# A fused attention and gated feed-forward kernel: logit sums by accumulating transfers instead of matmuls, first weights in halves, last store from ScalarE

## The chip, the core and the metric

The kernel runs on one core of a Trainium2 chip. Five engines run their own instruction streams, each strictly in its own order: TensorE (PE, matmuls into PSUM; PEld is its weight load), VectorE (DVE), ScalarE (ACT), GpSimd (POOL) and SyncE (SP). SP, ScalarE and GpSimd also issue transfers (DMA), which 16 DMA engines carry out. Engines wait for one another by semaphores. The metric is the device time of the program in microseconds; smaller is better.

## The reference

x is 2048 rows of 512. xn is its LayerNorm, and the result is x + s * g: s is a local dilated attention of xn with 32 heads of 16, g is silu of a gated feed-forward of xn.

```python
    W, dil = 8, 2
    qkv = (xn @ wqkv) ...                        # q, k, v: 32 heads of 16
    idx = pos[:, None] - arange(W) * dil         # position, and 2, 4, .. 14 before it
    logits = einsum("bhsd,bhswd->bhsw", q, kg) * scale      # masked below position 0
    attn = softmax(logits)                        # over the 8 places
    s = einsum("bhsw,bhswd->bhsd", attn, vg) ... @ wo
    g = silu((gelu(xn @ w_gate) * (xn @ w_up)) @ w_down)    # 512 -> 1792 -> 512
    return x + s * g
```

## The kernel before

The 2048 positions are four blocks of 512 (`TQ`, block j), each of four tiles of 128. Python functions record operations (`self.op(name, engine, duration, needs, emit, ...)`), each with estimated duration, the operations that it needs, buffers that it takes and a priority. `schedule` (line 75) then plays a list scheduler over them: at each step it picks the operation that can start first on its engine, by priority among those within 0.05 us, and so fixes each engine's order and the slot of every buffer. The order of `PARAMS` (lines 55 to 60) enters by per-stage base priorities and a seeded jitter. The program is then emitted in that order; on the chip each engine follows its own stream and waits for its semaphores.

For each block: `layernorm` (222) takes mean and variance (by ScalarE for the blocks in `sums`, else by DVE), normalizes, and turns the block to features x positions (`xnT`), by PE for block 0 and by transposing transfers from SP for the others. `qkv` (418; `qkv_tiles`, 503, for block 0) makes q, k and v. v goes through DRAM (`vT_dram`) and comes back with 4 x 32 partitions, quadrant tq holding the 32 heads of the tile tq of the block (`v_loads`, 562). `scores` (582) multiplies q with eight shifted windows of k on DVE: the four chunks c of q and k hold four of the 16 head features each, a head on four neighbouring partitions. Two levels of adds on DVE (`ladd`) sum the four chunks. What is left is a sum over the four partitions of each head, which PE does as a matmul with a 128x32 matrix of ones (`ind`):

```python
nc.tensor.matmul(
    L[H * tq : H * (tq + 1), w2, :], lhsT=self.ind[:],
    rhs=self.t[f"pr{j}_{w2}_{c}"][:, :, tq * P : (tq + 1) * P],
```

Eight such matmuls a block (line 640) fill two PSUM banks (pool "L"), laid out as 4 quadrants of 32 heads. The max over the eight places (`peak`), the subtraction (`less`), the exponential, its sum, reciprocal and scaling follow (656 to 690). `values` (708) multiplies the weights with eight windows of v and adds the products pairwise on DVE, one of the sums as an accumulating transfer from GpSimd (725). `turned` (849) takes the result through DRAM to features x positions, and `out` (871) multiplies it with wo (`s_ps`, line 883), multiplies with silu of the feed-forward, adds x and stores. `ffn` (752) makes the gate (`g_ps`) and up (`u_ps`) products with gelu, copies and products into `hT`; `down` (808) multiplies with w_down (`y_ps`, line 823) and takes silu. PSUM has eight banks: six in pool "F" that all matmul groups share, two for the logit sums. `loads` (964) issues all loads from SP but the second half of the first x tile.

Of the kernel before, what the change touches and what calls it, by code (L numbers as in the profile page):

```python
# [39 lines left out]
TABLE = 1.29  # L40
START = 0.8
LAT = {"PE": 0.2, "DVE": 0.1, "ACT": 0.13, "POOL": 0.15}
DEPENDENT = 0.115
DMA_FIXED = 2.3
DMA_CROWDED = 3.5
LOADED = 42.0
DMA_RATE = {"SP": 325e3, "POOL": 180e3}

POOLS = {"F": 6, "L": 1, "q": 2, "k": 2, "pr": 9, "attn": 2, "Ls": 1, "v": 2, "o": 1, "oT": 1, "h": 1,
         "xT": 2, "gl": 3, "sil": 1, "s16": 1, "xn": 4, "vst": 4}  # L50


DMA_SUMS = {(0, 0)}

PARAMS = dict(
    sums=(2, 3), ladd=2, ln_act=3, warm=4, slack=2.94, jitter=(9069, 1.0), N=[-49.4, -9.8, 21.5, 188.1],
    S=[108.2, -30.7, 42.8, 79.5], V=[-15.6, 90.4, 135.0, 139.5], Q=[-51.4, 66.2, 79.4, 143.2],
    F=[-41.0, 82.0, 126.2, 195.4], Y=[60.3, 103.2, 181.0, 249.0], O=[41.6, 84.1, 218.1, 258.6],
# [3 lines left out]
class Op:  # L62
    __slots__ = ("name", "eng", "dur", "need", "emit", "take", "use", "prio", "table", "bytes",
                 "start", "done", "end", "n", "slack", "mode")

    def __init__(self, name, eng, dur, need, emit, take=(), use=(), prio=0.0, table=None, nbytes=0,
                 slack=0.0, mode="full"):
# [4 lines left out]
        self.mode = mode  # L72


def schedule(ops, pools):
# [3 lines left out]
    for i, o in enumerate(ops):  # L79
        o.n = i  # L80
        waits[o.name] = len(o.need)
        for d in o.need:
            nexts[d].append(o.name)
# [10 lines left out]
    wire = {"SP": 0.0, "POOL": 0.0}  # L94
# [7 lines left out]
    while any(ready.values()):  # L102
# [31 lines left out]
        if o.bytes:  # L134
            clock[e] = t + o.dur
            wire[e] = max(wire[e], t + o.dur / 2) + o.bytes / DMA_RATE[e]
            end = wire[e] + DMA_FIXED + (DMA_CROWDED if e == "POOL" and t < LOADED else 0.0)
# [11 lines left out]
        o.done = end if o.bytes else clock[e] + (DEPENDENT if e == "DVE" else 0.0)  # L149
# [7 lines left out]
        for n in nexts[o.name]:  # L157
            waits[n] -= 1
            if not waits[n]:
                at[n] = max(  # L160
                    by[d].done if by[d].eng == by[n].eng else by[d].end + by[n].slack for d in by[n].need
                )
                ready[by[n].eng].append(by[n])
# [4 lines left out]
class Kernel:  # L168


    def __init__(self, par=PARAMS):
        self.par = par
        self.ops = []
        self.t = {}
        self.sums = {}
# [46 lines left out]
    def layernorm(self, j):  # L222
        base = self.when("N", j)
        for tt in range(TPB):
            t = j * TPB + tt
            prio = base + 2.0 * tt if j else -50.0 + tt
# [5 lines left out]
            def aggr(t=t):  # L232
                nc = self.nc
                nc.vector.bn_aggr(out=self.mv[:, t, :], in_=self.stats[:, t, :])

# [8 lines left out]
            def shift(a, b):  # L244
                self.nc.vector.scalar_tensor_tensor(
                    out=self.nmr[:, a:b, 0], in0=self.mv[:, a:b, 0], scalar=-1.0, in1=self.rstd[:, a:b, 0],
                    op0=ALU.mult, op1=ALU.mult,
                )
# [14 lines left out]
            def norm_dve(t=t):  # L263
# [4 lines left out]
                    scalar2=self.rstd[:, t, :], op0=ALU.subtract, op1=ALU.mult,  # L268
# [16 lines left out]
            def copy(t=t, tt=tt, j=j):  # L285
# [3 lines left out]
                if t == 1:  # L289
# [7 lines left out]
            by_act = j in self.par["sums"]  # L297
            if by_act:
# [14 lines left out]
                self.op(f"aggr{t}", "ACT", 0.70, [f"mean{t}"], square, prio=prio)  # L313
            else:
                self.op(f"stats{t}", "DVE", 0.61,
                        [f"ld_x{t if j == 0 else j}_{j}"] + {1: ["aggr0"], 2: ["copy1"]}.get(t, []), stats, prio=prio,
                        slack=(0.0, 0.5, 3.0, 3.0)[j])
                self.op(f"aggr{t}", "DVE", 0.16, [f"stats{t}"], aggr, prio=prio)
            on_act = j > 0 or t >= self.par["ln_act"]
# [6 lines left out]
            else:  # L326
                a, b = j * TPB, (j + 1) * TPB
                if tt == 0:
# [4 lines left out]
                    self.op(f"rstd{j}_", "POOL", 3.0, need,  # L333
                            lambda f=power, a=a, b=b, k=1.0 / D if by_act else 1.0: f(a, b, k), prio=prio, slack=0.5)
                ready = f"rstd{j}_"
            if on_act:
                self.op(f"norm{t}", "ACT", 0.75, [ready], norm_act, take=[("xn", f"xn{t}")],
                        use=[f"xn{t}"], prio=prio, slack=3.0 if j else 0.0)
            else:
                self.op(f"norm{t}", "DVE", 0.34, [ready], norm_dve, take=[("xn", f"xn{t}")],  # L340
                        use=[f"xn{t}"], prio=prio)
            if j:

                def cross(t=t, tt=tt, j=j):
                    if tt == 0:
# [5 lines left out]
                self.op(f"copy{t}", "SP", 0.8, [f"norm{t}"] + ([f"copy{t - tt}"] if tt else []), cross,  # L351
                        take=[("xT", f"xT{j}")] if tt == 0 else [], use=[f"xn{t}", f"xT{j}"], prio=prio,
                        nbytes=P * D * 2)
# [5 lines left out]
            self.op(f"copy{t}", *(("DVE", 0.34) if t == 1 else ("ACT", 0.5)), need, copy, take=take, use=[f"tr{t}", f"xT{j}"], prio=prio)  # L359

    def first_tile(self):
# [30 lines left out]
        def copy(i):  # L392
# [3 lines left out]
            self.nc.scalar.activation(out=out, in_=self.t[f"tr0_{i}"][:], func=AF.Copy)  # L396
# [14 lines left out]
        self.op("copy0", "ACT", 0.28, ["turn0_1", "copy0_0"], lambda: copy(1), use=["tr0_1", "xT0"], prio=prio)  # L411
# [6 lines left out]
    def qkv(self, j):  # L418
# [6 lines left out]
        for which, c in groups:  # L425
# [45 lines left out]
            if which == 2:  # L471
# [7 lines left out]
                self.op(f"stv{j}_{c}", "POOL", 1.0, [f"ev_{key}"], store, use=[f"vst{j}_{c}"], nbytes=128 * 1024)  # L479
# [23 lines left out]
    def qkv_tiles(self, base):  # L503

        for t in range(TPB):
            for which in range(3):
                key = f"{'qkv'[which]}0_t{t}"

                def mms(t=t, which=which, key=key):
                    ps = self.new("ps_" + key, [P, NC, P], F32, "qkv_ps")  # L510
                    for c in range(NC):
                        for dk in range(NC):
# [3 lines left out]
                                start=(dk == 0), stop=(dk == NC - 1),  # L516
# [19 lines left out]
                def store(t=t):  # L536
# [5 lines left out]
                self.op(f"mm_{key}", "PE", NC * NC * MM128, [f"copy{t}", f"ld_w{'qkv'[which]}"], mms,  # L542
                        take=[("F", "ps_" + key)], use=["ps_" + key, "xT0"],
                        prio=base + (0.5 if (t, which) == (1, 0) else t * 2 + which if which < 2 else 8 + t))
# [12 lines left out]
                if which == 2:  # L557
                    self.op(f"stv0_{t}", "POOL", 1.0, [f"ev_v0_{t}"], store, use=[f"vst0_{t}"],
                            nbytes=128 * 1024)
        self.v_loads(0)  # L560

    def v_loads(self, j):
        for tq in range(TPB):
# [10 lines left out]
            need = [f"stv{i}_{c}" for i in (j - 1, j) if i >= 0 for c in range(NC)]  # L574
            if j == 0:
                need = [f"stv0_{t}" for t in range(tq + 1)]
            need += [f"ldv{j}_0"] if tq else []
            self.op(f"ldv{j}_{tq}", "POOL", 1.0, need, load, take=[("v", f"v{j}")] if tq == 0 else [],
                    use=[f"v{j}"], prio=1.0, nbytes=290 * 1024)


    def scores(self, j):
        base = self.when("S", j)
        ladd = self.par["ladd"]
        sums = {}
        k = 0
        for w2 in range(2):
            for c in range(NC):


                cuts = [(0, 2), (2, 4)] if j == 0 and w2 == 0 else [(0, 4)]
                before = []
                for a, b in cuts:

                    def prod(j=j, w2=w2, c=c, a=a * P, b=b * P):
                        nc = self.nc
                        if a == 0:
                            self.new(f"pr{j}_{w2}_{c}", [P, 4, TQ], BF16, "prod")
                        off = PAD - HALO + 8 * w2 + a
                        win = self.t[f"k{j}"][:, c, off : off + b - a]  # L600
                        win = bass.AP(tensor=win.tensor, offset=win.offset, ap=[win.ap[0], [2, 4], [1, b - a]])
                        nc.vector.tensor_tensor(  # L602
                            out=self.t[f"pr{j}_{w2}_{c}"][:, :, a:b],
                            in0=self.t[f"q{j}"][:, c, a:b].unsqueeze(1).to_broadcast([P, 4, b - a]),
                            in1=win, op=ALU.mult,
                        )

                    need = [f"halo{j}"] + [f"ev_{n}{j}_{i}" for n in "qk" for i in ([c] if j else range(b))]
                    name = f"prod{j}_{w2}_{c}" + ("h" if b < TPB else "")
                    self.op(name, "DVE", 1.135 if b - a == 4 else 0.603, need + before, prod,  # L610
                            take=[("pr", f"pr{j}_{w2}_{c}")] if a == 0 else [],
                            use=[f"pr{j}_{w2}_{c}", f"q{j}", f"k{j}"], prio=base + k)
                    before = [name]
                k += 1

            def add(a, b, j=j, w2=w2):
                pa, pb = self.t[f"pr{j}_{w2}_{a}"], self.t[f"pr{j}_{w2}_{b}"]
                self.nc.vector.tensor_tensor(out=pa[:], in0=pa[:], in1=pb[:], op=ALU.add)  # L618

            tiles = [(c, f"prod{j}_{w2}_{c}") for c in range(NC)]  # L620
            step = 1
            for level in range(ladd):
                nxt = []
                for i in range(0, len(tiles), 2):
                    (a, na), (b, nb) = tiles[i], tiles[i + 1]
                    nm = self.op(f"ladd{j}_{w2}_{level}_{a}", "DVE", 1.135, [na, nb],
                                 lambda a=a, b=b, f=add: f(a, b),
                                 use=[f"pr{j}_{w2}_{a}", f"pr{j}_{w2}_{b}"], prio=base + k - 3)
                    nxt.append((a, nm))
                tiles = nxt  # L630

            sums[w2] = tiles

        def reduce(j=j):
            nc = self.nc
            L = self.new(f"L{j}", [P, 2, TQ], F32, "L_ps")
            for w2 in range(2):
                for i, (c, _) in enumerate(sums[w2]):
                    for tq in range(TPB):
                        nc.tensor.matmul(  # L640
# [489 lines left out]
```

## Time and profile before

| what | value |
|---|---|
| median of 3 runs (216.15 to 216.32) | 216.17 us |
| the profiled execution | 216.41 us |
| its span, first to last instruction | 214.7 us |
| granted TensorE clock | 1.0 throughout |
| first projection matmul starts | 6.31 us |
| last matmul ends | 210.57 us |
| instructions of PE, DVE, ACT, POOL | 1132, 216, 269, 69 |

The profile describes one execution. Busy time of an engine is the time in which it ran an instruction; the chain of waits follows back from the last instruction to what released it, at each step, and so names the work that the time consists of. A group of instructions is those of one line, engine and form, with the mean duration of one. For transfers, the time from issue to landing is given.

### The profile page before, as it was taken

How to read it: one execution, taken by the hardware profiler on the slowest of the kernel's cores; microseconds unless marked ns; L12 is line 12 of the kernel's file. 1: busy time of each engine (PE TensorE's matmuls, PEld its weight loads, DVE VectorE, ACT ScalarE, POOL GpSimd, SP SyncE). 2: the span in 40 equal slices, each digit the busy share in tenths (PEclk: the TensorE clock that was granted, in tenths of full speed). 3: DMA queues.
4: the chain of work that ended last, by engine and by line, in shares of the span. 5: the costliest groups of instructions: out<-in, count | busy, mean ns of one | idle time of the engine just before them, and what ended most of it. 6: DMA issues, size and time to landing. Idle time of an engine off the chain costs nothing.

```text
span 214.7 us, 3046 instructions
## 1 busy us (share of the span) xinstructions
PE 208.4 (97%) x1132; PEld 100.8 (47%) x1132; DVE 182.0 (85%) x216; ACT 156.4 (73%) x269; POOL 36.7 (17%) x69
## 2 busy tenths in 40 slices
PE   6999999999999999999999999999999999999992
PEld 2896444444544444444444444444444444444441
DVE  4598995599999999999999999999998799953033
ACT  3588999999998989877519967776724987765241
POOL 5036310034044312230200001001350010001000
PEclk9999999999999999999999999999999999999999
DMA  5999999204322401680297019303635540026712
GB/s 145 360 380 375 312 288 215 52 0 85 61 49 101 108 24 39 134 208 2 50 180 161 3 22 164 108 0 66 175 114 102 144 83 18 0 37 159 172 49 77
DMA packets 30575, 25.88 MB, mean 121 GB/s; under 512 B 16208, under 2 KB 28640, under 8 KB 30560
## 3 DMA queue, kind: packets, MB, share of 16 engines
q1 hardware_dynamic: 27584, 17.50, 31.4%
q0 software_dynamic: 2832, 8.11, 17.4%
q8 instruction: 9, 0.15, 0.3%
q14 instruction: 6, 0.05, 0.1%
q10 hardware_dynamic: 144, 0.07, 0.1%
HBM read 14.12 MB, written 6.31 MB: 95 GB/s over the span
## 4 chain that ended last, share of the span: by engine, by line
PE 93%; DMA 3%; SPq 1%; DVE 0%; ACT 0%; issue 0%; DVEq 0%
PE y_ps L823 23%; PE g_ps L763 23%; PE u_ps L763 23%; PE qkv_ps L432 15%; PE s_ps L883 6%; PE qkv_ps L513 3%; DMA wv_sb<-in_A_wqkv_dram 3%; PE L_ps L640 1%; SPq L968 1%; SPq L980 0%; DVE s L934 0%; ACT sil L838 0%; PE tr_ps L283 0%; DVE s L940 0%; DVEq L1125 0%
## 5 line engine op out<-in xcount | busy, mean ns | idle before, releaser
L763 PE MATMUL g_ps<-xnT,wg_sb 128*128 128x512 bf16 x224 | 56.0, 379 | 0.0
L763 PE MATMUL u_ps<-xnT,wu_sb 128*128 128x512 bf16 x224 | 55.4, 379 | 0.0
L823 PE MATMUL y_ps<-wd_sb,hT 128*128 128x512 bf16 x224 | 50.3, 379 | 0.0
L779 ACT ACTIVATE gl<-g_ps 128x512 bf16<-128x512 f32 x56 | 33.3, 602 | 9.7 <-PE g_ps L763 9.3
L602 DVE TENSOR_TENSOR prod<-q_sb,k_sb 128x2048 bf16<-128x2048 bf16 (+1 forms) x36 | 38.3, 1096 | 1.5 <-ACT k_sb L529 1.1
L787 ACT ACTIVATE hT<-u_ps 128x512 bf16<-128x512 f32 x56 | 33.2, 603 | 8.0 <-PE u_ps L763 7.9
L713 DVE TENSOR_TENSOR pv<-attn,v_arr 128x2048 bf16<-128x2048 bf16 x32 | 37.9, 1216 | 0.0
L823 PEld LDWEIGHTS <-hT 128*128 128x128 bf16 x224 | 21.7, 98 | 26.8 <-issue 0.8
L763 PEld LDWEIGHTS <-wu_sb 128*128 128x128 bf16 x224 | 21.9, 98 | 26.1
L763 PEld LDWEIGHTS <-wg_sb 128*128 128x128 bf16 x224 | 21.8, 98 | 26.2 <-issue 0.4
L618 DVE TENSOR_TENSOR prod<-prod 128x2048 bf16<-128x2048 bf16 x24 | 28.8, 1215 | 0.0
L721 DVE TENSOR_TENSOR pv<-pv 128x2048 bf16<-128x2048 bf16 x20 | 24.3, 1214 | 0.2
L801 DVE TENSOR_TENSOR hT<-hT,gl 128x1024 bf16<-128x1024 bf16 x28 | 19.0, 681 | 5.7 <-ACT hT L787 3.1
L838 ACT ACTIVATE sil<-y_ps 128x512 bf16<-128x512 f32 x16 | 9.4, 603 | 16.4 <-PE y_ps L823 16.3
L883 PE MATMUL s_ps<-wo_sb,oT_sb 128*128 128x512 bf16 (+2 forms) x68 | 15.0, 366 | 0.0
L897 ACT ACTIVATE s<-s_ps 128x512 bf16<-128x512 f32 x15 | 9.0, 597 | 5.7 <-PE s_ps L883 5.7
L569 POOL DMA_DIRECT2D v_arr<-vT_dram x16 | 10.5, 661 | 13.0 <-DMA vT_dram<-vst 12.8
L432 PE MATMUL qkv_ps<-xnT,wk_sb 128*128 128x512 bf16 x48 | 12.3, 379 | 0.0
L432 PE MATMUL qkv_ps<-xnT,wq_sb 128*128 128x512 bf16 x48 | 12.0, 379 | 0.0
L432 PE MATMUL qkv_ps<-xnT,wv_sb 128*128 128x512 bf16 x48 | 11.2, 379 | 0.0
L910 POOL DMA_DIRECT2D s<-x_sb x3 | 2.6, 875 | 50.1 <-DVE s L907 50.1
L274 ACT ACTIVATE xn<-x_sb,nmr,rstd 128x512 bf16<-128x512 bf16 x13 | 10.3, 827 | 0.0
(85 smaller groups left out, 196.6 us busy)
## 6 DMA issues: line engine op xcount, KB each, us to landing
v_arr<-vT_dram POOLq DMA_DIRECT2D x16, 142.0 KB, 4.0
vT_dram<-vst POOLq DMA_DIRECT2D x16, 128.0 KB, 2.3
pv<-pv POOLq DMA_DIRECT2D x4, 512.0 KB, 5.2
oT_dram<-o_sb SPq DMA_DIRECT2D x16, 128.0 KB, 2.8
oT_sb<-oT_dram SPq DMA_DIRECT2D x4, 512.0 KB, 3.6
wg_sb<-in_B_w_gate_dram SPq DMA_DIRECT2D x2, 896.0 KB, 10.8
wu_sb<-in_B_w_up_dram SPq DMA_DIRECT2D x2, 896.0 KB, 12.7
wd_sb<-in_B_w_down_dram SPq DMA_DIRECT2D x1, 1792.0 KB, 20.5
```

The costliest lines, as they stand in the source:

```text
L432: self.nc.tensor.matmul(ps[:], lhsT=self.w_qkv(which, dk, c), rhs=self.t[f"xT{j}"][:, dk, :], start=(dk == 0), stop=(dk == NC - 1),)
L569: self.nc.gpsimd.dma_start(out=self.t[f"v{j}"][H * tq : H * (tq + 1), :, :], in_=self.vT.rearrange("(h d) s -> h d s", d=DH)[:, :, a : a + ...
L602: nc.vector.tensor_tensor(out=self.t[f"pr{j}_{w2}_{c}"][:, :, a:b], in0=self.t[f"q{j}"][:, c, a:b].unsqueeze(1).to_broadcast([P, 4, b - a] ...
L618: self.nc.vector.tensor_tensor(out=pa[:], in0=pa[:], in1=pb[:], op=ALU.add)
L713: self.nc.vector.tensor_tensor(out=pv[:], in0=self.t[f"at{j}"][:, w, :].unsqueeze(1).to_broadcast([P, DH, P]), in1=self.t[f"v{j}"][:, :, 2 ...
L721: self.nc.vector.tensor_tensor(out=out[:], in0=pa[:], in1=pb[:], op=ALU.add)
L763: nc.tensor.matmul(ps[:], lhsT=w[:, dk, fc * P : (fc + 1) * P], rhs=self.t[f"xT{j}"][:, dk, :], start=(dk == 0), stop=(dk == NC - 1),)
L779: self.nc.scalar.activation(out=self.t[f"gl{j}_{pair}"][:, fc % 2, :], in_=self.t[f"ps_g{j}_{fc}"][:], func=AF.Gelu_apprx_tanh,)
L787: self.nc.scalar.activation(out=self.t[f"h{j}"][:, fc, :], in_=self.t[f"ps_u{j}_{fc}"][:], func=AF.Copy)
L801: self.nc.vector.tensor_tensor(out=h, in0=h, in1=self.t[f"gl{j}_{pair}"][:], op=ALU.mult)
L823: nc.tensor.matmul(self.t["ps_" + key][:, 0 : n1 - n0], lhsT=self.t[f"h{j}"][:, fc, tt * P : (tt + 1) * P], rhs=self.wd_sb[:, fc, n0:n1], ...
L883: self.nc.tensor.matmul(ps[:, 0 : n1 - n0], lhsT=self.t[f"oT{j}"][:, c, tt * P : (tt + 1) * P], rhs=self.wo_sb[:, c, n0:n1], start=(c == 0 ...
```

## The change

- `scores` is split. `logits` orders the products by halves of the block (n2: two tiles of 128) with all eight places in one instruction, instead of by halves of the places; three adds a half leave one tile `pr{j}_{n2}_0`. `reduced` is the matmul way of before, used for block 0 alone (`psum=(0,)`). `gathered`, for blocks 1 to 3, sums over the four partitions of a head by transfers from GpSimd: for each quadrant, four transfers of every fourth partition (32 x 1024 bf16) into `Ls` (32 partitions of fp32), the first a plain write, the other three accumulating. `peak` and `less` then read `Ls` in SBUF, in place.
- `values` makes four products of double width instead of eight; the accumulating transfer sums the two halves of the first.
- The first two y tiles of each block share the two banks of pool "L" as one tile (`shared=True`).
- Wq, wk and wv are loaded in halves, wq's from ScalarE's queue; w_down in two parts. In block 0, tile 0, the q and k matmuls are recorded as two operations of two feature chunks each, which need the halves. The second half of the first transposed tile is copied by DVE instead of ScalarE; tile 1's statistics are taken in halves.
- Block 2's mean and variance move from ScalarE to DVE (`sums=(3,)` instead of `(2, 3)`).
- The two last, narrow stores: the 192-wide one is issued from ScalarE. The stores of blocks 0 to 2 are halved.
- The scheduler's estimates of transfers get a fixed delay and a shared time for each kind (`LAG`, `WORK`), a need with "~" waits for a start only, the prod pool has 5 slots of double size instead of 9, the base priorities are new, and instead of the jitter a list of 840 numbers (`nudge`) shifts the priority of each operation. With them every engine's order changes.

```diff
 PARAMS = dict(
-    sums=(2, 3), ladd=2, ln_act=3, warm=4, slack=2.94, jitter=(9069, 1.0), N=[-49.4, -9.8, 21.5, 188.1],
+    sums=(3,), warm=4, slack=2.52, N=[-9.4, 354.1, -120.2, 179.5], psum=(0,), shared=True, rpow=True,
...
+    vnorm=(), vcopy=(1,), vsum=(0,), crowd=1.35,
+    nudge=[
...
+    def gathered(self, j):
+        base = self.when("S", j)
+        for tq in range(TPB):
+            before = [f"ladd{j}_{tq // 2}"] + (["~gat%d_0_0" % j] if tq else [])
+            for s in range(NC):
+                def gather(tq=tq, s=s):
+                    if tq == s == 0:
+                        self.new(f"Ls{j}", [P, W, P], F32, "Ls")
+                    self.nc.gpsimd.dma_start(
+                        out=self.t[f"Ls{j}"][H * tq : H * (tq + 1)],
+                        in_=self.t[f"pr{j}_{tq // 2}_0"][s::NC, 0, tq % 2],
+                        **(dict(accum_op=ALU.add) if s else {}),
+                    )
+                nm = self.op(f"gat{j}_{tq}_{s}", "POOL", 0.65, before, gather,
+                             take=[("Ls", f"Ls{j}")] if tq == s == 0 else [],
+                             use=[f"pr{j}_{tq // 2}_0", f"Ls{j}"], prio=base + 0.1 * s, nbytes=64 * 1024, kind="gat")
+                before = [nm]
...
+    def reduced(self, j):
+            for w2 in range(2):
+                for tq in range(TPB):
+                    pr = self.t[f"pr{j}_{tq // 2}_0"][:, 0, tq % 2, 4 * w2 : 4 * w2 + 4]
+                    self.nc.tensor.matmul(
+                        L[H * tq : H * (tq + 1), w2, :], lhsT=self.ind[:],
+                        rhs=pr.rearrange("p w t -> p (w t)"), start=True, stop=True,
+                    )
...
     def values(self, j):
+                out=pv[:], in0=self.t[f"at{j}"][:, 2 * i : 2 * i + 2, :].unsqueeze(2).to_broadcast([P, 2, DH, P]),
+                in1=win, op=ALU.mult,
...
     def down(self, j):
+                            if tt == 0:
+                                self.new(f"ps_y{j}", [P, 2, D], F32, "y_ps")
+                            self.t["ps_" + key] = self.t[f"ps_y{j}"][:, tt, :]
...
-                    self.nc.sync.dma_start(
+                    (self.nc.scalar if n0 else self.nc.sync).dma_start(
                         out=self.out2d[t * P : (t + 1) * P, n0:n1], in_=self.t[f"s16{j}"][:, tt, n0:n1]
...
+        wq = [("ld_wqa", lambda: w_qkv(0, 0, h, "scalar"), 256 * kb), ("ld_wq", lambda: w_qkv(0, h, NC, "scalar"), 256 * kb)]
+        wk = [("ld_wka", lambda: w_qkv(1, 0, h), 256 * kb), ("ld_wk", lambda: w_qkv(1, h, NC), 256 * kb)]
+        wv = [("ld_wva", lambda: w_qkv(2, 0, h), 256 * kb), ("ld_wv", lambda: w_qkv(2, h, NC), 256 * kb)]
-        seq = x0 + [wt[0], wt[1], xt[2], xt[3], wt[2], xb[1]]
+        seq = x0 + wq + wk + [xt[2], xt[3]] + wv + [xb[1]]
...
-    seed, spread = par["jitter"]
-    rng = random.Random(seed)
-    for o in k.ops:
-        if o.eng in ("PE", "DVE", "ACT") and o.prio > -40.0:
-            o.prio += spread * (2.0 * rng.random() - 1.0)
+    if par.get("nudge"):
+        for o, d in zip(k.ops, par["nudge"], strict=True):
+            o.prio += d / 10
```

More of the change, by code (lines that the diff above doesn't have):

```diff
@@ L572, in load @@
                 )
-            need = [f"stv{i}_{c}" for i in (j - 1, j) if i >= 0 for c in range(NC)]
+            need = [f"st_v{i}_{c}" for i in (j - 1, j) if i >= 0 for c in range(NC)]
             if j == 0:
[L576 to L582, printed above, removed]
+                need = [f"st_v0_{t}" for t in range(tq + 1)]
@@ L583, in scores, with logits @@
+            need += [f"~ldv{j}_0"] if tq else []
+            self.op(f"ldv{j}_{tq}", "POOL", 0.7, need, load, take=[("v", f"v{j}")] if tq == 0 else [],
+                    use=[f"v{j}"], prio=1.0, nbytes=290 * 1024, kind="ld")
+    def logits(self, j):
         base = self.when("S", j)
-        ladd = self.par["ladd"]
-        sums = {}
         k = 0
-        for w2 in range(2):
+        for n2 in range(2):
             for c in range(NC):
[L591 to L613, printed above, removed]
-                k += 1
[L616 to L632, printed above, removed]
@@ new lines, in logits, with within @@
+                need = [f"halo{j}"] + [f"ev_{n}{j}_{i}" for n in "qk" for i in ([c] if j else range(2 * n2 + 2))]
+                self.op(f"prod{j}_{n2}_{c}", "DVE", 1.135, need + ([f"prod{j}_{n2}_{c - 1}"] if c % 2 else []), prod,
+                        take=[("pr", pair)] if c % 2 == 0 else [], use=[pair, f"q{j}", f"k{j}"], prio=base + k)
+                k += 1
+            def within(n2=n2, i=0):
+                pr = self.t[f"pr{j}_{n2}_{i}"]
+                self.nc.vector.tensor_tensor(out=pr[:, 0], in0=pr[:, 0], in1=pr[:, 1], op=ALU.add)
```

334 lines of the change are left out of this document (217 added, 117 removed), and 41 rows, old and new, of the table nudge.

## The prediction

> **What bounds the kernel now.** I read the page's busy shares, then the chain of waits in order of time, then busy time by stage, then the timelines of both ends, and last the rows of transfers issued from GpSimd, because the change adds 48 of those. Busy shares:
>
> ```profile
> PE 208.4 (97%) x1132; PEld 100.8 (47%) x1132; DVE 182.0 (85%) x216; ACT 156.4 (73%) x269; POOL 36.7 (17%) x69
> ```
>
> The chain in order of time (start, length, what): it is TensorE almost without a break from the arrival of wv to the last output group.
>
> ```profile
> 3.77 6.43 DMA wv_sb<-in_A_wqkv_dram
> 10.25 1.07 PE qkv_ps L513 x16
> ...
> 75.65 0.55 PE L_ps L640 x8
> 76.19 1.83 PE qkv_ps L432 x8
> ...
> 209.73 0.60 ACT sil L838
> 210.36 0.75 DVE s L934 x2
> 211.12 0.23 DVE s L940
> 211.35 0.17 DVEq L1125
> ```
>
> Busy time by stage (window, its length, then PE, PEld, DVE, ACT, POOL):
>
> ```profile
> 5.40:42.80 37.40, 36.99 (x328) 22.67 (x328) 29.27 (x48) 33.23 (x66) 8.22 (x11) 1.00 1.02 284
> 42.80:97.90 55.10, 55.10 (x262) 25.70 (x260) 54.33 (x56) 49.59 (x90) 15.49 (x23) 1.00 0.35 79
> 97.90:154.60 56.70, 56.70 (x269) 26.01 (x268) 56.59 (x58) 38.27 (x60) 4.59 (x6) 1.00 0.41 82
> ```
>
> So the time is the first projection matmul (6.31 us), plus PE's work, plus a tail of 4.1 us (PE ends at 210.57, the span at 214.7). VectorE has no idle time either from 42.8 to 154.6 (0.9 us of 111.8). A matmul that goes away shortens the end one for one; a DVE wait in the middle has no idle DVE time to hide in, only the distance that the order leaves between a DVE result and its PE reader.
>
> **What is removed.** In blocks 1, 2 and 3 the eight L_ps matmuls go. Each group costs 0.55 us on the chain, and the piece behind it is longer than its matmuls need: 1.83 for 8 that take 8 x 0.216 = 1.73 elsewhere on the chain, likewise 0.11 behind each of the other two groups. 3 x 0.55 + 0.10 + 0.11 + 0.11 = 1.97 us. Block 0 keeps its group. The rest of PE's work is the same in number and shape (876 matmuls 512 wide, 192 projections 128 wide).
>
> **The start.** The first projection could begin when the first half of xnT is copied (the first of the two L396 copies ends at 5.85) instead of at 6.31, 0.4 us sooner. But PE then meets wv earlier: q and k of tiles 0 and 1 are 4 x 0.89 plus 0.22 of transposes, 3.8 us, so it would want wv at 9.7, and wv landed at 10.2 (3.77 + 6.43). Its place in SP's queue is no earlier, since wk now goes in two issues (0.43 to 0.51 us each) where wq and wk stood; the bytes ahead of it are the same. It can land up to 0.45 earlier, one issue, because ScalarE issues wq. The second half of wq stands in ScalarE's order behind a table load (1.28) and a 0.2 us activation, so it is issued near 0.8 + 0.4 + 0.43 + 1.28 + 0.2 = 3.1, against 1.73. Its landing lies between 2.3 us (the 64 KB x tile) and 6.4 us (wv, 512 KB) after that, 5.4 to 9.5, and PE wants it at 6.35. I take 6.6 (half of wq's own bytes, wq took 4.5): the 0.25 us wait is covered by the wait for wv. Sum for the start: -0.2, bounds -0.45 and +2.9.
>
> **The tail.** Today 0.86 us of short s_ps matmuls run behind the last y_ps matmul, beside its silu; in the new order 0.33 is left behind it, so the silu, two gates and two adds (about 1.8 us from the last y_ps in both) reach 0.5 further past PE's end. The last store was queued on SP until 211.8, 0.28 us after the last add at 211.52; now the 192-wide store leaves from ScalarE and the last one finds SP free. Landing of 128 KB instead of 48 KB is 1.7 against 1.6. +0.5 - 0.28 + 0.1 = +0.3.
>
> **What is added: 48 gathers.** They are 16 a block: four steps for each of four quadrants, three of them accumulating onto the one before, so the steps of a quadrant wait for each other's landing. All are issued from GpSimd, in one queue with the v loads, v stores, the pv sum and the residual sum. No trace shows a 32-row bf16-to-fp32 accumulation. The nearest rows:
>
> ```profile
> v_arr<-vT_dram POOLq DMA_DIRECT2D x16, 142.0 KB, 4.0
> vT_dram<-vst POOLq DMA_DIRECT2D x16, 128.0 KB, 2.3
> pv<-pv POOLq DMA_DIRECT2D x4, 512.0 KB, 5.2
> ```
>
> Issue: 0.55 us is the median of the plain stores (0.54 to 0.65), 0.88 of the pv accumulation with four times the rows; I take 0.6, as it is nearer to the plain ones in rows. Step, issue to landing: 2.1 to 2.3 at least (the store writes the same 128 KB), 5.2 at most (the only accumulating row, four times the bytes). The accumulation's excess of 2.9 over the store, a quarter of it for a quarter of the bytes, gives 3.0; I take 2.7.
>
> What has to cover them is the DVE work that stands, in the new order, between the last cell sum (the second add of prod tiles) and the first reader of the gathered sums, by the mean of each row (prod 1.19, add 1.2, geglu 0.68, a pv of double width 2 x 1.18):
> - Block 1, up to its max: 8 prods 9.5, 4 adds 4.8, 4 geglu 2.7, a gate 1.2 = 18.2. Needed: 16 issues 9.6, one v store and three v loads between them 2.5, the last landing 1.9 = 14.0 (by steps, 4 x 2.7 + 1.8 = 12.6). 4 us to spare.
> - Block 2: the first reader is not its max but a prod of block 3, which takes over a prod buffer that the gathers read. Ahead of it stand totals 1.4, reciprocal 0.95, geglu 0.68, share 0.68, 3 double pv 7.1, 3 adds 3.6, 2 prods 2.4 = 16.8. In GpSimd's queue the pv sum stands after the seventh gather and waits 6.1 us for its pv; with its 0.9 issue, quadrant 3 starts its last three steps at 7.0: 7.0 + 3 x 2.7 = 15.1. 1.7 us to spare.
> - Block 3: 6 geglu 4.1, reciprocal 0.95, share 0.68, 3 double pv 7.1, 4 adds 4.8 = 17.6. Needed: 12 issues and 4 v loads 9.8, landing 1.9 = 11.7.
>
> At 2.7 nothing waits, and with issues of 0.88 the sums become 18.5, 16.8 and 15.1, still level. At 4.0 block 2 needs 19.0 and DVE is 2.2 late there; at 5.2 the three blocks need 22.6, 22.6 and 21.4, 4.4 + 5.8 + 3.8 = 14.0 late. Behind a waiting gather stand the v loads of the next block and the v stores; behind a waiting DVE stand the geglu products that PE's y_ps and the PSUM banks wait for.
>
> **What moves.** Block 2's LayerNorm sums go from ScalarE to DVE: 4 x (0.64 + 0.20 + 0.73 + 0.20) = 7.1 us less there, 4 x (0.67 + 0.17) + 0.16 = 3.5 more on DVE. In the new order they stand before block 0's max, the stretch 5.4 to 42.8 in which DVE idles 8.1 us; without that cover they would cost 3.5. The pv products of double width, the max and subtract from SBUF instead of PSUM keep their element counts: nothing, as 1.22 us for 128x1024 fp32 and 0.59 ns an element for bf16 are lane rates here; a form that fell to half rate would cost 32 x 1.19 + 16 x 2.37 = 76 us, and only the extra dimension of the pattern is new (inner runs of 128 stand in today's pv). The first two y tiles of each block now sit in the two L banks, so block 0's y waits for its subtraction: 0.66 plus five PE groups 4.3 = 5.0 us after the group's start, against 0.55 + 0.2 + 0.29 + 1.22 + 0.68 + 1.22 + 0.1 = 4.3 for DVE: covered by 0.7. The second half of w_up, needed later today, is now needed behind 12 projection groups (10.7 us), three transposes (0.7), nine g and u groups (7.8) and 0.5 of waits from 5.9 on, at 25.6; it landed at 23.2 (9.03 + 14.2).
>
> **Sum.** -1.97 - 0.2 + 0.3 = -1.9 on the profiled execution's 216.41, 214.5; that run is 0.24 above the median of the runs shown (216.17), so 214.3, with 213.5 to 215.3 for the bounds of the start and for PE waits of some tenths.
>
> **Rivals.**
> 1. *Gathers of about 4 us.* For it: the v loads, also 32 rows and several in flight, take 4.0. Against: those move 512 pieces from DRAM, a gather 32 rows. DVE is 2.2 late in block 2, the gain is eaten in part or whole: 215.3 to 216.5.
> 2. *DVE waits become the bound (slower).* Steps like the accumulating row, 5.2 us, put the three places 14.0 us late; it decides from about 4.1 us, where the lateness passes the 1.9 gained. DVE has no idle time there, but the order leaves distance to PE, so half reaches it: 214.3 + 7 = 221. For it: three of four gathers accumulate. Against: a quarter of the bytes.
> 3. *GpSimd's issues are shut out by VectorE.* Each waits out a running DVE instruction, 1.2 us: 16 x (0.6 + 1.2) = 28.8 plus landing against covers of 17 to 18, 13 late a block, some 39, half of it on PE: 234. Against: 12 stores were issued in 0.54 to 0.65 beside a busy DVE; for: the 128x4 power on GpSimd took 1.0 to 1.9. The Trainium skill (SBUF — State Buffer, section "SBUF: two separate sides") says that transfers issued from GpSimd starve while DVE holds the shared port in a two-port mode; by that rule it is this rival, and the store rows of this trace do not bear it out.
> 4. *The split weights start worse.* The second half of wq lands at 9 instead of 6.6 and PE idles for up to 2.9: 215.3 to 217.2.
>
> **How the numbers follow.** Forecast 0.68; rival 1 0.14, rival 2 0.12, rival 3 0.01, rival 4 0.05. A measurement of this kernel tells no change from one of 0.2% (215.74 to 216.60). Faster: the forecast, 0.07 of rival 1 and 0.02 of rival 4, 0.77. Same: 0.06 of rival 1, 0.02 of rival 4, 0.08. Slower: the rest, 0.15. The range, 213.4 to 216.6, holds the forecast, rival 1 and most of rival 4, and leaves out rivals 2 and 3 and a few hundredths below.
>
> **What would show it.** Right: L_ps x8 on PE, PE busy from about 5.9 to 208.7 without a DMA or DVE wait past 11 us, gathers landing in under 3.3 us, the last store from SP at once. Wrong: DVE's max or prod waiting for a DMA onto Ls, PE idle before y_ps or u_ps at 100 to 175 us, or PE waiting for wq behind its first half.

## The result and the profile after

The changed kernel takes 223.75 us (median of 4 runs, 222.96 to 224.33) where the kernel before takes 216.25 (216.15 to 216.32, 4 runs): a ratio of 1.0345, 95% interval 1.0304 to 1.0386. The forecast was 214.3. The profiled execution of the changed kernel took 222.96.

Its page, the busy shares and some rows of the 40 slices (5.5 us each, tenths):

```profile
span 221.1 us, 3034 instructions
...
PE 208.2 (94%) x1089; PEld 101.2 (46%) x1108; DVE 186.0 (84%) x207; ACT 148.6 (67%) x252; POOL 73.1 (33%) x117
...
PE   6999999999999999999899999299999999989992
...
PEclk9999999999999999999999999769999999999999
DMA  6999997113052619889798660047997009914912
```

PE falls to 2 tenths in slice 26 and to 8 in two others, the granted clock drops in the two slices behind the hole, and the transfer engines are 7 to 9 tenths busy in slices 16 to 22 and 28 to 31, which is where most of the gathers run. The chain of waits, first its shares by engine before the change, then after it, then a few of its pieces after it in order of time (start, length, what):

```profile
PE 93%; DMA 3%; SPq 1%; DVE 0%; ACT 0%; issue 0%; DVEq 0%
```
```profile
PE 33%; DVE 31%; DMA 19%; POOL 8%; issue 5%; ACT 3%; ACTq 0%; DVEq 0%; POOLq 0%
```
```profile
82.01 2.93 DMA Ls<-prod
...
99.09 4.29 DMA Ls<-prod
103.40 1.89 DVE peak L788
...
117.28 6.52 DMA Ls<-prod
125.71 4.04 DMA Ls<-prod
```

Before, PE alone was 93% of this chain. Now, in blocks 1 to 3, it runs from a cell sum on DVE through the gathers to the first operation of DVE that has to wait for them, the maximum in blocks 1 and 3 and a product in block 2. VectorE's own timeline at the three places (start, length, instruction, in brackets the idle time before it and what ended that):

```profile
103.40 1.89 DVE L788 TENSOR_REDUCE peak<-Ls 128x128 f32<-128x1024 f32 x1 [3.69 <-DMA Ls<-prod]
...
129.83 1.22 DVE L700 TENSOR_TENSOR prod<-q_sb,k_sb 128x2048 bf16<-128x2048 bf16 x1 [3.68 <-DMA Ls<-prod]
...
165.96 1.91 DVE L788 TENSOR_REDUCE peak<-Ls 128x128 f32<-128x1024 f32 x1 [1.43 <-DMA Ls<-prod]
```

DVE is 3.7, 3.7 and 1.4 us late, 8.8 in all. The second place is the one that the prediction named, a product of block 3 that takes over a buffer the gathers still read. What PE lost by it (window, length, then PE, PEld, DVE, ACT, POOL, granted clock, DMA share, GB/s):

```profile
104.00:130.00 26.00, 24.81 (x115) 11.63 (x115) 22.04 (x21) 15.09 (x24) 14.53 (x20) 1.00 0.91 150
130.00:148.00 18.00, 14.00 (x54) 5.76 (x54) 18.00 (x18) 11.39 (x17) 3.58 (x6) 0.81 0.20 53
```
```profile
142.45:147.30 4.85, 4.85 (x12) 1.72 (x12) 4.85 (x8) 4.26 (x7) 2.75 (x4) 0.50 0.36 68
```

PE idles 1.2 us in the first window and 4.0 in the second, and 1.8 in other windows of the same kind between 12 us and its end: 7.0. Not all of it comes from the gathers. PE's timeline has four gaps of 0.4 us and more behind its start: 0.43 at 58 us, ahead of any gather and also there in the run with only the first steps below, and 1.08 (up to 105.95), 3.95 (up to 142.45) and 0.58 (up to 194.59), which that run does not have. These three are 5.6 us. Behind the 3.95 us hole the clock stands at 0.50 for 4.85 us, which by estimate costs another 2.4 (half of 4.85). Together 8.0, of the 8.7 by which the stretch from PE's first projection to its last matmul (5.7 to 217.2, 211.5 us) is longer than forecast (5.9 to 208.7, 202.8).

The way from late VectorE to idle PE at the largest hole leads through ScalarE:

```profile
140.86 1.06 ACT L807 ACTIVATE attn<-Ls 128x1024 bf16<-128x1024 f32 x1 [5.60 <-DVE Ls L794]
141.82 2.53 ACT L927 ACTIVATE hT<-u_ps 128x512 bf16<-128x512 f32 x5
142.45 1.86 PE L903 MATMUL u_ps<-xnT,wu_sb 128*128 128x512 bf16 x4 [3.95 <-ACT hT L927]
```

Block 2's exponential stands in ScalarE's order ahead of five reads of finished u_ps tiles. It waits 5.6 us for the late subtraction, and PE waits for those reads.

The transfers themselves (KB each, median us from issue to landing; then the issuing instructions' shortest, median and longest in ns, and the same for landing):

```profile
Ls<-prod POOLq DMA_DIRECT2D x48, 128.0 KB, 3.9
```
```profile
L776 POOL DMA_DIRECT2D Ls<-prod x48: 512/874/1757, 82.0 to 161.1; - x48
...
DMA to landing us min/median/max: 2.8/3.9/6.5
```

A step takes 3.9 us at the median where the prediction took 2.7, and its issue 0.87 where it took 0.6.

### The profile page after: what moved, and what is told of

It is laid out like the page before. It is cut to its first block, busy times and chain, and to the rows that moved or that the text cites. A ratio compares the mean times of both kernels' runs of the same rounds, so it can differ in the third digit from the quotient of the medians.

```text
span 221.1 us, 3034 instructions
## 1 busy us (share of the span) xinstructions
PE 208.2 (94%) x1089; PEld 101.2 (46%) x1108; DVE 186.0 (84%) x207; ACT 148.6 (67%) x252; POOL 73.1 (33%) x117
## 4 chain that ended last, share of the span: by engine, by line
PE 33%; DVE 31%; DMA 19%; POOL 8%; issue 5%; ACT 3%; ACTq 0%; DVEq 0%; POOLq 0%
DMA Ls<-prod 17%; PE y_ps L967 10%; DVE prod L700 7%; PE g_ps L903 6%; PE u_ps L903 6%; DVE pv L846 6%; POOL Ls L776 6%; PE qkv_ps L607 5%; DVE prod L712 4%; PE s_ps L1031 3%; DVE prod L716 3%; DVE peak L788 3%; PE qkv_ps L523 2%; DMA wq_sb<-in_A_wqkv_dram 2%; DVE pv L853 2%
## 5 line engine op out<-in xcount | busy, mean ns | idle before, releaser
L903 PE MATMUL u_ps<-xnT,wu_sb 128*128 128x512 bf16 x219 | 53.8, 384 | 4.2 <-ACT hT L927 4.0
L967 PE MATMUL y_ps<-wd_sb,hT 128*128 128x512 bf16 x219 | 52.3, 379 | 2.4 <-DVE hT L941 1.1
L776 POOL DMA_DIRECT2D Ls<-prod x48 | 38.5, 946 | 36.3 <-DMA Ls<-prod 11.3
L919 ACT ACTIVATE gl<-g_ps 128x512 bf16<-128x512 f32 x56 | 31.5, 597 | 17.4 <-PE g_ps L903 13.3
L700 DVE TENSOR_TENSOR prod<-q_sb,k_sb 128x2048 bf16<-128x2048 bf16 x32 | 37.9, 1220 | 4.0 <-DMA Ls<-prod 3.7
L846 DVE TENSOR_TENSOR pv<-attn,v_arr 128x4096 bf16<-128x4096 bf16 x16 | 36.2, 2283 | 0.1
L712 DVE TENSOR_TENSOR prod<-prod 128x2048 bf16<-128x2048 bf16 x16 | 19.2, 1219 | 0.0
L1058 POOL DMA_DIRECT2D s<-x_sb x3 | 3.2, 1056 | 35.4 <-DVE s L1055 35.4
L672 POOL DMA_DIRECT2D v_arr<-vT_dram x16 | 13.4, 881 | 3.7 <-DMA vT_dram<-vst 3.7
L853 DVE TENSOR_TENSOR pv<-pv 128x2048 bf16<-128x2048 bf16 x12 | 14.4, 1219 | 0.0
L807 ACT ACTIVATE attn<-Ls 128x1024 bf16<-128x1024 f32 x4 | 4.2, 1057 | 11.5 <-DVE Ls L794 11.5
```

What stands on the lines that cost most here:

```text
L700: self.nc.vector.tensor_tensor(out=self.t[pair][:, c % 2].rearrange("p n w t -> p w n t"), in0=q.unsqueeze(1).to_broadcast([P, W, 2, P]), ...
L712: self.nc.vector.tensor_tensor(out=pr[:, 0], in0=pr[:, 0], in1=pr[:, 1], op=ALU.add)
L776: self.nc.gpsimd.dma_start(out=self.t[f"Ls{j}"][H * tq : H * (tq + 1)], in_=self.t[f"pr{j}_{tq // 2}_0"][s::NC, 0, tq % 2], **(dict(accum_ ...
L846: self.nc.vector.tensor_tensor(out=pv[:], in0=self.t[f"at{j}"][:, 2 * i : 2 * i + 2, :].unsqueeze(2).to_broadcast([P, 2, DH, P]), in1=win, ...
L853: self.nc.vector.tensor_tensor(out=pv[:, 0], in0=pv[:, 0], in1=pv[:, 1], op=ALU.add)
L903: nc.tensor.matmul(ps[:], lhsT=w[:, dk, fc * P : (fc + 1) * P], rhs=self.t[f"xT{j}"][:, dk, :], start=(dk == 0), stop=(dk == NC - 1),)
```

## The experiments

Times are medians; ratios are to runs of the kernel before on the same chip (216.28, 216.12 and 216.15 us in the three groups).

**Only the first step of each quadrant.** Does the new order cost the time, or the chains of accumulating steps?

```diff
-                    self.nc.gpsimd.dma_start(
+                    if s == 0:
+                        self.nc.gpsimd.dma_start(
...
```

> The changed kernel without the 36 accumulating steps: each quadrant keeps its first, plain transfer (12 in all), so the logits are one partition's share and not the sum over four. Every engine's order but GpSimd's is unchanged. If the chains of accumulating steps are what costs (theory), the waits of DVE's max and of its prod on Ls (5.1 and 3.7 us) are gone, PE has no stretch of more than 0.5 us idle between 12 and 210 us, the granted clock is 1.0, and the time is 213.8 to 215.5. If the new order of the engines is at fault whatever the sums cost (rival), PE still idles for some 4 us near 135 us and the time stays above 219. The max should stay at 1.9 us if it is the place of its operand (SBUF), and fall to 1.2 if it was slowed by the transfers beside it.

Measured: 214.75 us (214.31 to 216.54), ratio 0.9924 [0.9891, 0.9957]. PE's slices, and the twelve first steps that are left (KB, median us to landing):

```profile
PE   7999999999999999999999999999999999999992
...
Ls<-prod POOLq DMA_DIRECT2D x12, 128.0 KB, 3.4
```

No slice of PE has a hole and no DVE instruction waits for Ls. (The profiled execution, 216.49, is 1.7 above the median.) With the order, the split weights and the stores unchanged, leaving 36 transfers out is worth 223.75 - 214.75 = 9.0 us, more than the 7.5 that the change lost. The new order works without the chains, so the chains are the cause; this run does not say what in them is.

**All steps plain.** The same 48 transfers, three of four no longer adding.

```diff
                         in_=self.t[f"pr{j}_{tq // 2}_0"][s::NC, 0, tq % 2],
-                        **(dict(accum_op=ALU.add) if s else {}),
```

> All 48 steps in the same order and with the same waits on one another, but each a plain write (bf16 to fp32) in place of three accumulating ones, so the logits are the last partition's share alone. If what makes a step long is the accumulation (reading the target and adding), issue falls from 0.85 to 0.52 us, a step from 3.9 to 2.9 us or less, which the covers of the prediction hold (block 2 needs 7.0 + 3 x 2.9 = 15.7 of 16.8): 214 to 216.5. If it is the four steps in a row and the number of transfers in flight (rival), a step stays at 3.5 us or more and the time stays above 219.

Measured: 219.21 us (218.35 to 219.61), 1.0123 [1.0076, 1.017]. Issues and landings, and the stretch in which block 2's gathers run (columns as above):

```profile
L776 POOL DMA_DIRECT2D Ls<-prod x48: 515/527/841, 82.4 to 158.0; - x48
...
DMA to landing us min/median/max: 2.5/3.5/5.7
```
```profile
106.00:128.00 22.00, 21.34 (x98) 10.01 (x99) 19.74 (x19) 12.79 (x20) 10.35 (x19) 1.00 0.98 180
```

The same window before the change:

```profile
106.00:128.00 22.00, 22.00 (x109) 9.72 (x108) 22.00 (x25) 15.35 (x23) 0.85 (x1) 1.00 0.50 96
```

The addition is worth 4.5 us (0.35 us an issue, 0.4 a step): the issue fell as the theory said, but the step stayed at 3.5 and the time above 219, as the rival said. The other 4.5, against the run with only first steps, remain without any addition, with the transfer engines at a share of 0.98 in place of 0.50. DVE is 4.7 us late at the same three places (1.95 and 0.73 at the maxima, 1.99 at the product, for which the profile names no releaser).

**Half the bytes.** `Ls` in bf16, so that the steps write and add 64 KB instead of 128 (the sums are rounded to bf16 after each step).

```diff
-                        self.new(f"Ls{j}", [P, W, P], F32, "Ls")
+                        self.new(f"Ls{j}", [P, W, P], BF16, "Ls")
```

> The sums are accumulated in bf16 instead of fp32 (target of 2 KB a partition instead of 4 KB, no cast); the max and the subtraction read and write bf16. If the bytes written and the cast set the step (theory A: 128 KB against 64 KB), a step falls from 3.9 towards 3.2 us and the time to 216 to 220; if it is the fixed cost of an accumulating step (theory B), it stays within 0.3 us of 3.9 and the time at 222 to 224, less what a faster max on bf16 may give (0.7 us at each of three places).

Measured: 216.75 us (216.13 to 219.08), 1.0036 [0.9995, 1.0078]. Issues and landings; VectorE's wait; the window as above:

```profile
L776 POOL DMA_DIRECT2D Ls<-prod x48: 522/1110/2147, 82.4 to 154.7; - x48
...
DMA to landing us min/median/max: 2.0/3.4/4.8
```
```profile
DVE peak L788 <- DMA Ls<-prod: 1.1, 2, 0.7
```
```profile
106.00:128.00 22.00, 21.89 (x101) 10.47 (x102) 20.75 (x19) 12.81 (x21) 14.61 (x20) 1.00 0.73 132
```

7.0 us come back though the median issue is 0.24 us longer than in the changed kernel and the order is the same. DVE is late by 2.0 us (0.75 and 0.31 at the maxima, 0.98 at the product). So the length of an issue doesn't set the result by itself. Compared with the plain fp32 steps, the landing is nearly the same (3.4 against 3.5) and the issue longer, yet the time is 2.5 us shorter, with the engines' share at 0.73 and not 0.98. This points at what the steps hold of the transfer engines; no run varies that alone. The queue of transfers issued from GpSimd (q0) gives its size: packets, MB and share, in the changed kernel, here and before:

```profile
q0 software_dynamic: 5136, 14.41, 32.9%
q0 software_dynamic: 4944, 11.26, 26.7%
q0 software_dynamic: 2832, 8.11, 17.4%
```

Times the spans of 221.1, 214.8 and 214.7 us, and with the other transfers of the queue taken as unchanged, the 48 gathers hold all 16 engines for 72.7 - 37.4 = 35.4 us in fp32 and 57.4 - 37.4 = 20.0 in bf16, 0.74 and 0.42 us each, 11.8 and 6.7 a block. (Against the run with only first steps, 20.8% of 214.8 us, the 36 accumulating ones alone come to 0.78 each.)

**One chain at a time.** Quadrant 0 keeps its four steps, the others only their first.

```diff
-                    self.nc.gpsimd.dma_start(
+                    if s == 0 or tq == 0:
+                        self.nc.gpsimd.dma_start(
...
```

> After with the accumulating steps of quadrants 1, 2 and 3 left out (27 transfers): each of blocks 1 to 3 has one chain of four steps (quadrant 0) and three single plain steps, so the sums of three quadrants lack three of their four products. The step is the same instruction as before, only alone. Theory (the step is long because four chains share the same 16 transfer engines, 0.78 us of all of them a step): alone, an accumulating step takes 2.6 to 3.0 us from issue to landing, near the shortest step seen with four chains, 2.8; no wait of DVE for Ls over 0.5 us, granted clock full, 214.0 to 215.3 us. Rival (an accumulating step has a latency of about 3.9 by itself, whatever else is in flight): median step of the chain 3.7 to 4.0, the chain of a block still 4 steps x 3.9 = 15.6 long, DVE waits of 1 to 3 us in blocks 1 and 2, 217 or more.

Measured: 215.2 us (214.45 to 216.51), 0.9944 [0.9911, 0.9977]; no wait of DVE for Ls. Seven accumulating steps stand singly in GpSimd's timeline. They land 3.4, 3.4, 3.2 us (block 1), 5.2, 3.2, 3.2 (block 2, the first while that block's plain steps were still landing) and 3.3 (block 3) after issue. The timeline in block 1 (idle time before it in brackets):

```profile
82.35 2.16 POOL L777 DMA_DIRECT2D Ls<-prod  x4 [6.30 <-DVE prod L716]
84.50 0.55 POOL L565 DMA_DIRECT2D vT_dram<-vst  x1
85.82 0.85 POOL L777 DMA_DIRECT2D Ls<-prod  x1 [0.77 <-DMA Ls<-prod]
89.50 0.84 POOL L777 DMA_DIRECT2D Ls<-prod  x1 [2.83 <-DMA Ls<-prod]
```

The time came out as the sharing theory said, the step between both theories: 3.2 to 3.4 alone, neither 2.6 to 3.0 nor 3.7 to 4.0. Half of the forecast's error in a step, 0.6 us, is there when the accumulating step stands alone; the rest, 0.6 at the median and more in block 2 (4.3 there), comes with the other chains. At 3.3 the prediction's own sum for block 2 is 7.0 + 3 x 3.3 = 16.9 against a cover of 16.8, so the step alone would hardly have been late. The run also takes 27 issues out of GpSimd's queue, so its time alone does not part the sharing of the transfer engines from the queue on GpSimd; the step does.

**The edges alone.** The kernel before with weights in halves (wq's from ScalarE) and the last narrow store from ScalarE.

```diff
-                    self.nc.sync.dma_start(
+                    (self.nc.scalar if n0 else self.nc.sync).dma_start(
...
-            eng = self.nc.sync
...
+            for a in (0, NC // 2):
+                (self.nc.sync if i else self.nc.scalar).dma_start(
...
```

> The kernel before, in its own order, with the two edges of the change alone: wq (from ScalarE), wk and wv in halves, with tile 0's q and k matmuls in two passes over the halves, and the 192-wide last store from ScalarE. By the prediction the start is set by wv (wait for it at 10.2 us) and the last store gains 0.28: 215.7 to 216.2. Rival: the second half of wq, issued behind the table load, makes PE wait: 216.4 to 218.

> e5 once more with more rounds, because its interval reached to both sides: the kernel before with the halved first weights and the last store from ScalarE. Its profile began the projections 0.4 us sooner, had no wait for wv, and ended 0.9 us sooner; if that holds in the mean, 215.3 to 215.8, a ratio of 0.996 to 0.998; if it was one execution's luck, 1.000.

Measured: 215.9 us (215.46 to 218.23), 1.0006 [0.997, 1.0041], and again 215.85 (215.55 to 218.24), 1.0002 [0.9974, 1.003]. Both medians lie about 0.3 below the kernel before, both intervals hold no change: inconclusive, and small in any case.

**Pairwise maxima on bf16.** With `Ls` in bf16 the maximum became the next thing to look at. It had been costed at the price it has from PSUM. The groups (line, engine, operation, count, then busy, mean ns, idle before) of the kernel before, the changed one, and the bf16 one:

```profile
L657 DVE TENSOR_REDUCE peak<-L_ps 128x128 f32<-128x1024 f32 x4 | 4.9, 1217 | 0.0
```
```profile
L788 DVE TENSOR_REDUCE peak<-Ls 128x128 f32<-128x1024 f32 x3 | 5.7, 1906 | 5.1 <-DMA Ls<-prod 5.1
```
```profile
L788 DVE TENSOR_REDUCE peak<-Ls 128x128 f32<-128x1024 bf16 x3 | 5.7, 1916 | 1.1 <-DMA Ls<-prod 1.1
```

1.91 us from SBUF in either type against 1.22 from PSUM, and 1.91 in the run with only first steps too, where no accumulating step competes: with this pattern it is the place of the operand. The reduction takes the maximum of eight values that lie 128 elements apart. The Trainium skill (SBUF — State Buffer, section "Door 1: The DMA port swizzle (why `[64,N]` ≈ `[32,N]`)") says that SBUF is read in 16-byte lines and that each access that goes to a new line pays; the SBUF rows agree with that. Of PSUM it says that lines are shorter and that patterns which are not contiguous slow matmuls; for this reduction the PSUM row, 1.22 for the same pattern, shows no such price. The edit replaces the one reduction by three pairwise maxima of contiguous rows, and the subtraction then reads their bf16 result in place of the fp32 `peak`:

```diff
-            self.nc.vector.tensor_reduce(
-                out=self.peak[:], in_=self.t[f"Ls{j}"][:].rearrange("p w t -> p t w"), axis=AX.X, op=ALU.max
-            )
+            src = self.t[f"Ls{j}"]
+            for half in (4, 2, 1):
+                self.nc.vector.tensor_tensor(
+                    out=self.top[:, 0:half, :], in0=src[:, 0:half, :], in1=src[:, half : 2 * half, :], op=ALU.max
+                )
+                src = self.top
```

> As e3 (sums accumulated in bf16, same order of every engine), with the max of blocks 1 to 3 as three pairwise maxima in bf16 (512, 256 and 128 wide) in place of the strided reduction of 1.9 us. If VectorE bounds the stretch in which the gathers lie, the three maxima together take about 1.0 us, 0.9 us less at each of three places, and the time falls by 1 to 2.5 us below e3, to 214.2 to 215.7. If the transfers alone decide there (rival), DVE only waits longer and the time stays within 0.5 us of e3's 216.75.

Measured: 214.72 us (214.49 to 214.86), 0.9926 [0.9899, 0.9952], faster than both kernels. PE's slices, the first of the three maxima and the subtraction (ns), and VectorE's wait:

```profile
PE   7999999999999999999999999999999999999992
```
```profile
L790 DVE TENSOR_TENSOR top<-Ls x3: 419/426/426, 100.9 to 157.3; 128x512 bf16<-128x512 bf16 x3
L797 DVE TENSOR_TENSOR Ls<-Ls,top x3: 683/684/684, 102.4 to 160.4; 128x1024 bf16<-128x1024 bf16 x3
```
```profile
DVE top L790 <- DMA Ls<-prod: 1.8, 2, 1.1
```

VectorE still waits 1.8 us for gathers, and 1.0 at the product, but PE no longer has a hole. The maximum costs 0.43 + 0.52 (the two smaller ones together, 258 ns each at the median) instead of 1.91, the subtraction 0.68 instead of 1.22: 1.5 us less a block, 4.5 in three, of which 2.0 reach the time: what VectorE does in the stretch counts beside the transfers. It is within 0.1 of the run without the accumulating steps.

**The order made anew for the measured costs.** Perhaps the order only had to know. The planner's figures for a gather are raised to what was measured, the priorities are searched again for the same instructions, in fp32 and (with the maxima) in bf16.

```diff
-LAG = {"turn": 1.1, "st": 0.9, "ld": 1.3, "sto": 1.3, "ldo": 1.35, "acc": 1.1, "gat": 1.4, "out": 0.75, "end": 1.1}
-WORK = {"turn": 0.8, "st": 0.42, "ld": 0.82, "sto": 0.6, "ldo": 1.8, "acc": 2.6, "gat": 0.3, "out": 0.8, "end": 0.05}
+LAG = {"turn": 1.1, "st": 0.9, "ld": 1.3, "sto": 1.3, "ldo": 1.35, "acc": 1.1, "gat": 1.7, "out": 0.75, "end": 1.1}
+WORK = {"turn": 0.8, "st": 0.42, "ld": 0.82, "sto": 0.6, "ldo": 1.8, "acc": 2.6, "gat": 0.92, "out": 0.8, "end": 0.05}
...
-                nm = self.op(f"gat{j}_{tq}_{s}", "POOL", 0.65, before, gather,
+                nm = self.op(f"gat{j}_{tq}_{s}", "POOL", 0.87 if s else 0.53, before, gather,
```

> The changed kernel with the same instructions (fp32 accumulating gathers, reduction for the max), but the scheduler told what the runs showed of them: issue 0.53 us plain and 0.87 accumulating, each step occupying the shared transfer engines for 0.92 us (measured 0.78, with a reserve), a longer fixed delay, 1.82 us for the max, and a new list of priority shifts found for these numbers. If the loss comes from an order that allowed the gathers too little (theory), PE has no idle stretch over 1 us and the time is 213.8 to 216.0. If 48 gathers cost time in any order, by contention with the other transfers or VectorE's own length (rival), it is 217 to 221.

> As e7, with sums accumulated in bf16 (0.60 us of the transfer engines a step told to the scheduler, measured 0.42) and the three pairwise maxima. If both terms add, 213.3 to 215.3, the fastest of all; if only the order mattered, equal to e7 within 0.5 us.

Measured: fp32 219.45 us (218.72 to 220.48), 1.015 [1.0118, 1.0182]; bf16 218.75 (218.53 to 219.28), 1.0116 [1.0088, 1.0143]. Both missed what was expected of them. VectorE's waits, first of the fp32 order, then of the bf16 one:

```profile
DVE peak L801 <- DMA Ls<-prod: 3.7, 2, 3.3
```
```profile
DVE prod L714 <- ACT k_sb L637: 5.2, 1, 5.2
```

In fp32 the new order recovers 4.3 of the 7.5 us, and the gathers still keep VectorE 3.7 waiting; v loads took 5.9 us instead of 4.2 and v stores 4.5 instead of 2.9, as if the room that the order gave the gathers was taken from other transfers; no run tests that. In bf16 it is 4.0 worse than the old order, with new waits elsewhere. Whether a better fp32 order exists is open: these two show only that this planner, told these figures, doesn't find one.

## Why the prediction was wrong

- **The failed step is the size of the gathers' need.** The covers were nearly right, the need was not. From the last cell sum to the point where DVE would go on, the trace has 18.0, 16.2 and 16.3 us in blocks 1, 2 and 3 (forecast 18.2, 16.8, 17.6); the sums were there after 21.7, 19.9 and 17.7 (forecast 14.0, 15.1, 11.7). "At 2.7 nothing waits" failed because a step was 3.9: the value was scaled from the medians of stores and of large accumulations that were issued one or a few at a time, and the 48 new transfers' own claim on the 16 shared engines was never added up. It was there to be had from the page of before: q0 held the engines for 17.4% of 214.7 us for 8.11 MB, 4.6 us a MB, so the gathers' 6.3 MB come to an estimated 29 us, near 10 a block (35.4 and 11.8 measured). The Trainium skill (DMA: Bandwidth & Descriptors, section "Rules for kernel authors") says of two transfers to disjoint partition halves that both spread over the same 16 engines and so serialize. Here it is four quadrants, and the shares of 0.91 and 0.98 above agree. Block 1 term by term, on GpSimd's timeline:

```profile
82.01 2.15 POOL L776 DMA_DIRECT2D Ls<-prod  x4 [6.31 <-DVE prod L716]
84.15 0.55 POOL L565 DMA_DIRECT2D vT_dram<-vst  x1
85.46 0.85 POOL L776 DMA_DIRECT2D Ls<-prod  x1 [0.77 <-DMA Ls<-prod]
86.68 3.38 POOL L776 DMA_DIRECT2D Ls<-prod  x4 [0.36 <-issue]
92.26 0.82 POOL L776 DMA_DIRECT2D Ls<-prod  x1 [2.21 <-DMA Ls<-prod]
92.80 1.60 POOL L672 DMA_DIRECT2D v_arr<-vT_dram  x2
94.17 3.69 POOL L776 DMA_DIRECT2D Ls<-prod  x4
97.01 1.50 POOL L672 DMA_DIRECT2D v_arr<-vT_dram  x1
98.18 2.03 POOL L776 DMA_DIRECT2D Ls<-prod  x2
```

  16 issues took 12.9 us (forecast 9.6), the store and the loads took 2.0 beyond what overlaps them (2.5), the queue stood idle for 3.3, all but 0.4 of it waiting for landings (0: either the issues or the steps were to decide, and both did, in turn), and the last landing, at 103.4, outlasted its issue by 3.2 (1.9). The sign that the prediction named for being wrong came: PE idle before y_ps (up to 105.95) and before u_ps (up to 142.45).
- **The rivals.** Rival 2's mechanism is what happened, at a step below its 5.2 and even below the 4.1 from which it was to decide. (By the prediction's own sum for block 2, 7.0 + 3 x 3.9 - 16.8, the lateness reaches the 1.9 gained at 3.9, not at 4.1. And the pv sum was not the only accumulating row: the residual sum, 512 KB too, took 5.0.) Rival 1 had the step almost right and gave 215.3 to 216.5, because it saw only block 2 late. The two shared the fault above: both moved the step and left the issues and the queue's waits as they were; rival 1 left block 1 as it was too.
- **"Half reaches PE", rival 2's rule, was a little low, and the clock was left out.** Of 8.8 us of DVE lateness 5.6 became idle time of PE that the run with only first steps doesn't have; by the rule of half it would have been 4.4. With plain steps it was 2.9 of 4.7 (gaps of 1.08, 0.82 and 0.96), in bf16 1.3 of 2.0 (0.38 and 0.96), so near two thirds each time. With the pairwise maxima, where VectorE had 4.5 us less to do, 2.8 us of waits left no such gap. The half clock behind the longest hole, 2.4, stood in no term of the prediction.
- **The maximum and the subtraction from SBUF at nothing:** the subtraction yes (1.22), the maximum no: 0.7 us more, three times, on an engine without slack.
- **The removal and the edges.** With only first steps the kernel is 1.5 us faster than before, with one chain 1.0, so the removal of the matmuls and the edges bring most of the 1.9 that was forecast, the longer maximum paid. The start: the second half of wq was issued at 1.8, not 3.1, and awaited until 6.3 (forecast 6.6); PE then didn't wait for wv, whose second half, issued at 4.6, landed 5.2 later at most, at 9.8, ahead of its first use at 9.96. The tail is 3.9 us (221.1 - 217.2) against 4.1 before and 4.4 forecast. GpSimd's issues were not shut out by VectorE: plain ones took 0.53 us beside a busy DVE, so rival 3 is out.

## What to carry to other kernels

When transfers are added, cost them twice: as a chain of landings, and as time of the shared transfer engines (queue share times span over count, for the nearest rows), summed over everything in flight in that stretch; if that sum comes near the cover, a single row's landing time is no guide. Near two thirds of the lateness of an engine without idle time became idle time of PE here, and the longest hole cost clock besides, so a gain of 2 us on PE did not pay for a reduction moved onto transfers that need 12 us of all engines a block. Halving their bytes (7.0 us back) did more than re-ordering around them (4.3), and only with VectorE's share of the work shortened too was the kernel faster than before. Price an operation whose operand moves from PSUM to SBUF as a new one, its pattern included.

## What was not expected of the hardware

- A maximum over rows 128 elements apart took 1.91 us from SBUF, in fp32 and in bf16, and 1.22 from PSUM; the subtraction of the same size took 1.22 from either.
- After PE had idled 3.95 us the granted clock stood at 0.50 for the next 4.85 us of matmuls; a hole of 1.1 us left it at 1.0.
- An accumulating transfer of bf16 onto bf16 had a longer issue than one onto fp32 (1.11 us median over all 48 gathers, against 0.87) though it landed sooner (3.4 against 3.9).
